# A decode kernel with its backward: the turn between the third and the last cache pass written out by 512 units, and the passes' openings in 1 MB requests

## The chip, the cores and the metric

The kernel runs on one core of a Trainium2 chip. The metric is the time of one execution on the device, in microseconds, as the median of several runs. Engines are called by the profile's names: PE (TensorE, matrix products), DVE (VectorE), ACT (ScalarE), POOL (GpSimd) and SP (SyncE, which here issues the loads).

## The reference

Two layers of a decoder work on one token of width D = 1024, with the same weights. Each layer is an attention over a cache of 65,536 positions (32 query heads, 4 key and value heads, head width 128) and a dense stage with a squared ReLU (F = 3584):

```python
x = x + attention(layernorm(x), k_cache, v_cache, wq, wo)     # softmax(q k / sqrt(128)) v, then wo
x = x + (relu(layernorm(x) @ w1 + b1) ** 2) @ w2 + b2
x = x + attention(layernorm(x), k_cache, v_cache, wq, wo)
x = x + (relu(layernorm(x) @ w1 + b1) ** 2) @ w2 + b2
out, vjp = jax.vjp(f, x, k_cache, v_cache, wq, wo, w1, b1, w2, b2)
return (out, *vjp(grad_out))
```

So the result is the output and the gradients with respect to x, both caches and all weights. The gradients of the caches alone have the caches' size (each cache is 64 MB in bfloat16).

## The kernel before, in words

The kernel reads both caches four times, in four passes numbered 0 to 3: pass 0 is the attention forward of the first layer, pass 1 that of the second, pass 2 the attention backward of the second layer, and pass 3 the backward of the first, which also stores the gradients of the caches. Between the passes lie turns, in which the dense weights are applied: the first turn between passes 0 and 1, the second between 1 and 2 (last forward and first backward through the dense stage), the third between 2 and 3. The code calls layers by L1 and L3 for attention and L2 and L4 for the dense stages.

All loads go into an arena of 20 granules of 1 MB (`Slot`). Some granules hold planes of scores or kept blocks of a cache across a turn, so in the third turn about five are free for weights.

**Cache loads.** A block of a cache is 1 MB. The helper `kv8` (L355 to L372) loads the block that the pass needs next. For an even block it first tries to take two adjacent granules and to load two blocks with one request of 2 MB (L370). If no two adjacent ones are free, or if the block's key stands in `KV["halves"]`, or in pass 3, it loads one block with a request of 1 MB (L365). `start_pass` (L425 to L431) fills that set with the last 8 blocks that the pass touches, and in passes after the first with the first 10. Inside a pass, the order on PE, DVE and ACT is the written one (`tc.manual_schedule`); SP's order of requests is the scheduler's, and each request waits on SP for its granule.

**Background.** Weights for the next head group are loaded and applied beside a pass. `by_group` says after how many items of a pass the work on the next group begins: at a quarter of a group's items (in pass 3, from the second on, 8 items in).

**The backward passes.** For each unit, `vS` multiplies the value block by the gradient of the attention's output (`dOT`), and adds the term of the softmax's backward with a matrix product of `sel2` and `ndt`, which is the first one into that PSUM bank (L1233 in pass 2).

**The turns.** The second turn is written out by hand: w1 comes in chunks of 512 columns of all 1024 rows (`ch_load`, L1674), seven of them, and for each chunk `ch_turn` transposes a part on PE, ACT or DVE copy the transposes out of PSUM (L1696), `ch_spread` (L1703, L1705) lays the 512 values of the hidden gradient out over the partitions, and `ch_dots` (L1712) does the remaining rows as dot products on DVE.

The third turn goes through a queue of rows, class `Rows`. Its `front` (L664 to L690) takes a row chunk of a weight and either forms a dot product on DVE (L673) or transposes it on PE (L682) and copies it out of PSUM with `evac`, on ACT (L161) or DVE (L164), whichever has the lower sum of the costs noted so far. Its `back` (L705 to L717) multiplies the transposed chunk with the vector (L714). Four weights go through it in turn, each as soon as the vector before it is known:

```python
rows.add(PRE["wq3"], DC, R, ..., fin_dx2, inplace=True)                  # dq of the last group -> dx2
rows.add(w2_slabs()[0], FC, DC, lambda: dx2[:], fin_dh2, mix=True, side=side_x4)
rows.add(w1_slabs()[0], DC, FC, lambda: dh2[:], fin_dx1, cols=f_cols, mix=True)
rows.add(wo_slabs(firstg[3])[0], R, DC, lambda: dx1[:], dO_finish(L1, firstg[3]), inplace=True)
rows.run()
```

All of w2 is used for dh2 before w1 is used for dx1. w1 is read by whole rows here. `side_x4` (L1833) uses the same w2 rows for the forward output of the last dense stage (x4). The order on all engines in this turn is the scheduler's. The next pass opens when `dOT` (L948) is there.

Of the kernel before, what the change touches and what calls it, by code (L numbers as in the profile page):

```python
# [16 lines left out]
P = 128  # L17
# [3 lines left out]
def kernel(  # L21
# [69 lines left out]
    def ps_sc(shape, dtype=F32):  # L91
        return PS["pool"].tile(shape, dtype, name="ps_sc", tag="sc", bufs=1 if PS["pass4"] else 2)
# [332 lines left out]
    def start_pass(p):  # L425
        KV["keep"] = plan_keep(p)
        KV["turned"] = KV.get("next", set())
        KV["next"] = set()
        KV["turn"] = {0: "k", 2: "v"}.get(p)
        NOW["pairs"] = p < 3  # L430
        KV["halves"] = set(TOUCH[p][-8:] + (TOUCH[p][:10] if p else []))  # L431

    def f_cols(ap, nb):
        return ap[:, bass.ds(512 * (nb // 4) + nb % 4, P, step=4)]
# [342 lines left out]
    class Background:  # L777
# [35 lines left out]
        def by_group(self, p, gen):  # L813

            order = list(dict.fromkeys(g for g, _ in ITEMS[p]))
            n = len(ITEMS[p]) // G
            for k, g in enumerate(order[1:]):
                self.later.append((k * n + 8 if PS["pass4"] and k else k * n + n // 4, gen(g), g))

        def drain(self):  # L820
            while self.later:
# [376 lines left out]
    def attn_bwd3(p, L, on_group, bg, end=()):  # L1198
        st = ExitStack()
        dspool = st.enter_context(tc.tile_pool(name="b3_ds", bufs=2))  # L1200
        items = ITEMS[p]
        dOpad = vec.tile([P, G, 8, R], BF, name="dOpad")
        nc.vector.memset(dOpad[:], 0.0)
        state = {}
        gfirst = {g: next(c8 for gg, c8 in items if gg == g) for g in range(G)}
        glast = {g: [c8 for gg, c8 in items if gg == g][-1] for g in range(G)}

        def vT(g, c8):
            bg.need(g)
            vb8 = kv8("v", g, c8)  # L1210
            if is_turned("v", g, c8):
                state[("vt", g, c8)] = vb8
            else:
                pt = ps_tr()
                for i in range(8):
                    nc.tensor.transpose(pt[:, i, :], vb8[:, i, :], ident_b[:, :])  # L1216
                kv_done("v", g, c8)
                vt = turned_to("v", g, c8, vb8)
                evac(vt[:, :, :], pt[:, :, :], kind="kta" if c8 % HB // 8 in ACT_VT else "kt")
                state[("vt", g, c8)] = vt  # L1220

        def vS(g, c8):
            if c8 == gfirst[g]:
                nc.vector.tensor_copy(out=dOpad[:, g, 0, :], in_=L["dOT"][:, gsl(g)])
                ndt = dspool.tile([64, HB, R], BF, name="ndt", tag="ndt")
                nc.vector.tensor_copy(out=ndt[:, :, :], in_=L["nd2"][:, gsl(g)].unsqueeze(1).to_broadcast([64, HB, R]))
                state["ndt"] = ndt
            vt = state.pop(("vt", g, c8))
            for i in range(8):
                s = (c8 + i) % HB  # L1230
                if s == 0:
                    state["ps_dp"] = ps_sc([P, HB, R])
                    nc.tensor.matmul(state["ps_dp"][:, :, :].rearrange("p c r -> p (c r)"), lhsT=sel2[:, :],  # L1233
                                     rhs=state["ndt"][:, :, :].rearrange("o c r -> o (c r)"), start=True, stop=False)
                w = min(8, HB - s)
                nc.tensor.matmul(state["ps_dp"][:, s:s + w, :].rearrange("p a b -> p (a b)"), lhsT=vt[:, i, :],
                                 rhs=dOpad[:, g, 0:w, :].rearrange("p a b -> p (a b)"), start=False, stop=(s == HB - 1))
            if is_turned("v", g, c8):
                kv_done("v", g, c8)
            if (c8 + 8) % HB == 0:  # L1240
                c0 = c8 + 8 - HB
                ps_dp = state["ps_dp"]

                def ds():
                    dsT = dspool.tile([P, HB, R], BF, name="dsT", tag="dsT")
                    nc.vector.tensor_tensor(out=dsT[:, :, :], in0=ps_dp[:, :, :], in1=E(1, g, c0, HB), op=ALU.mult)
                    add_load(dve=0.7)
                    state[("ds", g, c0 // HB)] = dsT
                after(1, ds)

        def k8(g, c8):
            kb8 = kv8("k", g, c8)
            dsT = state[("ds", g, c8 // HB)]
            if c8 % SU == 0:
                state["ps_dq"] = ps_acc([P, 8, R])
            ps_dq = state["ps_dq"]
            for i in range(8):
                c = c8 + i
                s = c % HB
                w = min(8, HB - s)  # L1260
                nc.tensor.matmul(ps_dq[:, 0:w, :].rearrange("p a b -> p (a b)"), lhsT=kb8[:, i, :],  # L1261
                                 rhs=dsT[:, s:s + w, :].rearrange("p a b -> p (a b)"),
                                 start=(c % SU == 0), stop=(c % SU == SU - 1), skip_group_check=True)
            kv_done("k", g, c8)
            if (c8 + 8) % SU == 0:
                su = c8 // SU

                def fold():
                    fold_dq(L, g, su, ps_dq[:, 0, :], gfirst[g] // SU == su, glast[g] // SU == su, dspool)
                    if glast[g] // SU == su:  # L1270
                        on_group(g)
                first_at(1, fold)

        start_pass(p)
        with tc.manual_schedule(engines=ORDERED):
            pipeline(items, [(vT, 0), (vS, TLEAD), (k8, B3_LAG)], bg, end)
        st.close()


    def attn_bwd4(p, La, Lb, on_group, bg, stack, end=()):  # L1280
# [75 lines left out]
        def vS(g, c8):  # L1356
# [3 lines left out]
            for i in range(8):  # L1360
                s = (c8 + i) % J
                if s == 0:
                    state["ps_dp"] = ps_sc([P, J, R2])
                    nc.tensor.matmul(state["ps_dp"][:, :, :].rearrange("p c r -> p (c r)"), lhsT=sel2[:, :],
                                     rhs=state["ndt"][:, :].unsqueeze(1).to_broadcast([64, J, R2]), start=True, stop=False)
                w = min(4, J - s)
                nc.tensor.matmul(state["ps_dp"][:, s:s + w, :].rearrange("p a b -> p (a b)"), lhsT=vt[:, i, :],  # L1367
                                 rhs=DOB[:, g, 0:w, :].rearrange("p a b -> p (a b)"), start=False, stop=(s == J - 1))
            if is_turned("v", g, c8):
                kv_done("v", g, c8)  # L1370
                if c8 % J == J - 8 and nexts:
# [326 lines left out]

    def ch_spread(s):

        pg = ps_tr([P, 512], F32)
        for j in range(4):
            nc.tensor.matmul(pg[:, j * P:(j + 1) * P], lhsT=dhb[:, 4 * s + j:4 * s + j + 1].to_broadcast([P, P]), rhs=ident_b[:, :],  # L1703
                             start=True, stop=True)
# [97 lines left out]
    def on3(g):  # L1802
        if g != lastg[2]:
            bg.add(g_dn(L3, dn3, g, g == firstg[2]))
    attn_bwd3(2, L3, on3, bg, [(10, pre_load("wq3", lambda: wq_slabs(lastg[2], 2)))])
    bg.drain()


# [2 lines left out]
    dx2 = vec.tile([P, DC], F32, name="dx2")  # L1811
    dh2 = vec.tile([P, FC], F32, name="dh2")
    dx1 = vec.tile([P, DC], F32, name="dx1")

    def fin_dx2(y):
        dn_finish(dn3, False)(y)
        dxn3 = ln_bwd(dn3[:], L3["n"], L3["rstd"])
        nc.vector.tensor_tensor(out=dx2[:], in0=dx3[:], in1=dxn3[:], op=ALU.add)

    def fin_dh2(y):  # L1820
        nc.vector.scalar_tensor_tensor(out=dh2[:], in0=y, scalar=2.0, in1=L2["r"][:], op0=ALU.mult, op1=ALU.mult)

    def fin_dx1(y):
        dxn = ln_bwd(y, L2["n"], L2["rstd"])
        nc.vector.tensor_tensor(out=dx1[:], in0=dx2[:], in1=dxn[:], op=ALU.add)
    rows = Rows(DENSE["pool"])
    rows.add(PRE["wq3"], DC, R, lambda: L3["dqT"][:, gsl(lastg[2])], fin_dx2, inplace=True)
    x4 = vec.tile([P, DC], F32, name="x4")
    ps_x4 = ps_acc([P, DC, 64])

    def side_x4(kc, slab):
        for nb in range(DC):
            nc.tensor.matmul(ps_x4[:, nb, :], lhsT=d_cols(slab, nb), rhs=L4["gb"][:, kc:kc + 1].to_broadcast([P, 64]),  # L1833
                             start=kc == 0 and nb == 0, stop=kc == FC - 1 and nb == DC - 1, skip_group_check=True)
        add_load(pe=DC * 0.03)
        if kc == FC - 1:
            f = tmp.tile([P, DC], F32, name="ffn_f")
            nc.vector.tensor_tensor(out=f[:], in0=ps_x4[:, :, 0], in1=b2c[:], op=ALU.add)
            nc.vector.tensor_tensor(out=x4[:], in0=x3[:], in1=f[:], op=ALU.add)
            col_to_dram(x4, D, out_0.rearrange("a b d -> (a b d)"))  # L1840
    rows.add(w2_slabs()[0], FC, DC, lambda: dx2[:], fin_dh2, mix=True, side=side_x4)
    rows.add(w1_slabs()[0], DC, FC, lambda: dh2[:], fin_dx1, cols=f_cols, mix=True)
    rows.add(wo_slabs(firstg[3])[0], R, DC, lambda: dx1[:], dO_finish(L1, firstg[3]), inplace=True)
    rows.run()
    dst.close()
    psA_stack.close()

# [90 lines left out]
```

## Time and profile before

| | |
|---|---|
| runs | 1949.32, 1951.35, 1955.88 us; median 1951.35 |
| profiled execution | 1954.17 us; span in the trace 1952.4 us, mean granted clock of TensorE 0.916 |
| busy | PE 82%, DVE 60%, ACT 54%, POOL 7% |
| data moved | 787.63 MB, 403 GB/s on average; 617.62 MB read, 165.69 MB written |
| first turn, us from the span's start | about 350 to 413, pass 1 opens behind it |
| second turn | about 745 to 786, pass 2 opens behind it |
| third turn | about 1128 to 1183, pass 3 opens at 1185.4 and ends at 1946 |
| in the third turn | dq 1127.97, dx2 1136.43, dn2 1177.2, dx1 1179.79, dOT 1183.14 |

The span runs from the first to the last instruction, and the execution's own time is 1.8 us longer. In the profile, a line such as L682 is a line of the kernel; "out<-in" names what an instruction writes and reads; "x152" is a count; and the idle time before a group is given with what ended it. GB/s is what all of the core's DMA engines moved in a stretch, and the DMA share how much of the stretch they were busy.

### The profile page before, as it was taken

The numbers are of one execution on the slowest core, as the hardware profiler recorded it, in microseconds if no ns is written. First come the engines' busy times: TensorE is split into PE (matmuls) and PEld (weight loads), VectorE is DVE, ScalarE is ACT, GpSimd is POOL, SyncE is SP. The second block draws the span as 40 slices with busy tenths as digits, with TensorE's granted clock in tenths as the row PEclk, the third lists the DMA queues.
The fourth block names the chain that finished last, engine by engine and source line by source line (L and its number), as shares of the span: only waits on it lengthen the run. The fifth ranks groups of instructions, "written<-read, shape, count | busy, mean of one in ns | idle before, by whom it ended". The sixth has DMA issues, their size and how long they took to land. (4 is left out here: it accounts for less than half of the span.)

```text
span 1952.4 us, 66978 instructions
## 1 busy us (share of the span) xinstructions
PE 1592.5 (82%) x30199; PEld 1304.0 (67%) x30199; DVE 1172.5 (60%) x2453; ACT 1044.6 (54%) x1617; POOL 141.8 (7%) x321
## 2 busy tenths in 40 slices
PE   6878788688878888877787888889987987787977
PEld 6868778587777777777776885555554554454544
DVE  5645555255545555545464576867875886676866
ACT  3434334254334446435363455766875785676765
POOL 0000000000000000000000001211211211121211
PEclk9999899699899999999899999988996998898997
DMA  9999999999999999899999988999999999899998
GB/s 395 426 426 427 426 428 413 397 398 424 429 425 428 427 423 304 333 425 428 427 423 418 408 309 302 416 405 406 424 423 420 401 424 412 355 423 392 424 422 318
DMA packets 105997, 787.63 MB, mean 403 GB/s; under 512 B 9312, under 2 KB 16494, under 8 KB 42094
## 3 DMA queue, kind: packets, MB, share of 16 engines
q1 hardware_dynamic: 81630, 617.65, 76.8%
q0 software_dynamic: 24080, 165.70, 20.4%
q8 instruction: 236, 3.87, 0.7%
q14 instruction: 51, 0.42, 0.1%
HBM read 617.62 MB, written 165.69 MB: 401 GB/s over the span
## 5 line engine op out<-in xcount | busy, mean ns | idle before, releaser
L164 DVE COPY kt<-ps_tr 128x1024 bf16<-128x1024 bf16 x724 | 497.0, 689 | 438.2 <-PE ps_tr L1024 244.6
L161 ACT CAST arena<-ps_gg 128x1024 bf16<-128x1024 f32 x457 | 444.5, 1011 | 194.7 <-PE ps_gg L1408 145.1
L1024 PE MATMUL ps_tr<-ident_b,arena 128*128 128x128 bf16 x3840 | 309.2, 225 | 32.3 <-DMA arena<-in_A_k_cache_dram 21.0
L164 DVE CAST arena<-ps_gg 128x1024 bf16<-128x1024 f32 (+2 forms) x186 | 222.4, 1196 | 86.4 <-PE ps_gg L1408 41.6
L161 ACT COPY kt<-ps_tr 128x1024 bf16<-128x1024 bf16 x164 | 171.3, 1052 | 186.5 <-PE ps_tr L1216 112.0
L1024 PEld LDWEIGHTS <-arena 128*128 128x128 bf16 x3840 | 233.5, 101 | 39.8 <-DMA arena<-in_A_k_cache_dram 23.4
L1126 PE MATMUL ps_acc<-arena 128*128 128x64 bf16 (+4 forms) x4096 | 205.8, 196 | 64.5 <-DMA arena<-in_A_v_cache_dram 51.9
L1408 PE MATMUL ps_gg<-GG,xt 64*128 64x512 bf16 x1024 | 212.8, 413 | 41.8 <-DVE arena L164 29.1
L1126 PEld LDWEIGHTS <-arena 128*128 128x128 bf16 x4096 | 159.9, 100 | 70.1 <-DMA arena<-in_A_v_cache_dram 55.6
L1336 PE MATMUL ps_tr<-ident_b,arena 128*128 128x128 bf16 x1824 | 178.5, 233 | 32.5 <-DMA arena<-in_A_v_cache_dram 30.5
L1107 ACT ACTIVATE arena<-S_sb,L_negm 128x128 bf16<-128x128 f32 x256 | 165.7, 1005 | 63.7 <-DVE L_negm L1092 63.7
L1042 PE MATMUL ps_sc<-L_qpad,kt 128*128 128x64 bf16 (+7 forms) x3584 | 183.5, 194 | 17.8 <-ACT kt L161 8.9
L1216 PE MATMUL ps_tr<-ident_b,arena 128*128 128x128 bf16 x1920 | 155.4, 227 | 42.6 <-DMA arena<-in_A_v_cache_dram 41.8
L1336 PEld LDWEIGHTS <-arena 128*128 128x128 bf16 x1824 | 118.0, 104 | 88.6 <-issue 54.0
L1042 PEld LDWEIGHTS <-kt 128*128 128x128 bf16 x3584 | 153.0, 100 | 22.6 <-ACT kt L161 11.8
L1216 PEld LDWEIGHTS <-arena 128*128 128x128 bf16 x1920 | 117.9, 102 | 46.6 <-DMA arena<-in_A_v_cache_dram 44.4
L1439 PEld LDWEIGHTS <-arena 128*128 128x128 bf16 x2048 | 95.1, 102 | 61.9 <-issue 42.2
L1107 ACT ACTIVATION_READ_ACCUMULATOR arena<-S_sb,L_negm 128x1 f32 x256 | 128.4, 502 | 0.0
L1408 PEld LDWEIGHTS <-xt 64*128 64x128 bf16 x1024 | 64.6, 94 | 87.9 <-issue 49.4
L587 ACT ACTIVATE mv_t<-mv_t 128x1024 bf16<-128x1024 bf16 x96 | 102.0, 1064 | 36.1 <-DVE mv_t L598 36.0
L1261 PE MATMUL ps_acc<-dsT,arena 128*128 128x64 bf16 (+7 forms) x2048 | 102.9, 194 | 16.1 <-DMA arena<-in_A_k_cache_dram 13.2
L1367 PE MATMUL ps_sc<-DOB,kt 128*128 128x64 bf16 (+3 forms) x1824 | 113.3, 198 | 0.0
(317 smaller groups left out, 2156.9 us busy)
## 6 DMA issues: line engine op xcount, KB each, us to landing
arena<-in_A_k_cache_dram SPq DMA_DIRECT2D x86, 2048.0 KB, 21.3
arena<-in_A_v_cache_dram SPq DMA_DIRECT2D x83, 2048.0 KB, 21.2
out_dram<-arena POOLq DMA_DIRECT2D x149, 1024.0 KB, 17.0
arena<-in_A_v_cache_dram SPq DMA_DIRECT2D x76, 1024.0 KB, 13.7
arena<-in_A_k_cache_dram SPq DMA_DIRECT2D x76, 1024.0 KB, 14.8
arena<-in_A_wo_dram SPq DMA_DIRECT2D x22, 1024.0 KB, 13.9
arena<-in_B_w_dram SPq DMA_DIRECT2D x21, 1024.0 KB, 9.1
arena<-in_A_wq_dram SPq DMA_DIRECT2D x18, 1024.0 KB, 13.6
```

The source lines that it names most:

```text
L161: nc.scalar.copy(out=out, in_=in_)
L164: nc.vector.tensor_copy(out=out, in_=in_)
L587: nc.scalar.activation(out=t[:, :], in_=t[:, :], func=ACTF.Copy, accum_out=y[:, kc:kc + 1])
L1024: nc.tensor.transpose(pt[:, i, :], kb8[:, i, :], ident_b[:, :])
L1042: nc.tensor.matmul(state["ps_s"][:, s:s + w, :].rearrange("p a b -> p (a b)"), lhsT=kt[:, i, :], rhs=L["qpad"][:, g, 0:w, :].rearrange("p ...
L1107: nc.scalar.activation(out=E(p, g, c0, SU)[:, :, h], in_=S[:, h, :], func=ACTF.Exp, bias=L["negm"][:, g, su, h:h + 1], scale=SCALE, accum_ ...
L1126: nc.tensor.matmul(ps_o[:, 0:w, :], lhsT=vb8[:, i, :], rhs=E(p, g, c, w), start=(c % SU == 0), stop=(c % SU == SU - 1), skip_group_check=True)
L1216: nc.tensor.transpose(pt[:, i, :], vb8[:, i, :], ident_b[:, :])
L1261: nc.tensor.matmul(ps_dq[:, 0:w, :].rearrange("p a b -> p (a b)"), lhsT=kb8[:, i, :], rhs=dsT[:, s:s + w, :].rearrange("p a b -> p (a b)") ...
L1336: nc.tensor.transpose(pt[:, i, :], vb8[:, i, :], ident_b[:, :])
L1367: nc.tensor.matmul(state["ps_dp"][:, s:s + w, :].rearrange("p a b -> p (a b)"), lhsT=vt[:, i, :], rhs=DOB[:, g, 0:w, :].rearrange("p a b - ...
L1408: nc.tensor.matmul(pg[:, 512 * h:512 * h + 512], lhsT=xt[64 * h:64 * h + 64, j1 // 8 + m, :], rhs=gg[64 * h:64 * h + 64, :, :].rearrange(" ...
```

## The change

- **Openings.** The list of blocks that passes 1 and 2 load in requests of 1 MB at their start grows from 10 to 18 (pass 3 has no pairs anyway).
- **The later group.** In passes 1 and 2 the background of the first next group begins at a half of the group's items instead of a quarter.
- **Late delta.** In `vS` of passes 2 and 3, for a group's first unit, the product of `sel2` and `ndt` comes last into its bank instead of first.
- **A bank.** `ch_spread` of the second turn takes its PSUM tile from another pool.
- **The third turn.** wq's rows are transposed in place at the end of pass 2 (`turn_wq`, 8 items before the end). The rest is written out in a `manual_schedule`. w2 comes in seven chunks of 512 rows and w1 in seven chunks of 512 columns, and they are loaded in turn, w2 first. For each chunk s, in this order: `back2` and `unite` give 512 values of dh2 (half of them from PE, half from dot products on DVE, and all from PE for the first chunk); `turn2` transposes the next chunk of w2; `spread1`; `dots2` of the next chunk; `back1` adds the chunk's part of dn2 for six of eight row blocks; `turn1` transposes the next chunk of w1, the last part of it copied by DVE; `dots1` does the other two row blocks on DVE; `x4_part` of the next chunk; then the granules are given back and `more` issues the next loads. x4 is finished after the rows of wo.

```diff
-        KV["halves"] = set(TOUCH[p][-8:] + (TOUCH[p][:10] if p else []))
+        KV["halves"] = set(TOUCH[p][-8:] + (TOUCH[p][:18] if p else []))
...
-                self.later.append((k * n + 8 if PS["pass4"] and k else k * n + n // 4, gen(g), g))
+                self.later.append((k * n + 8 if PS["pass4"] and k else k * n + n // (2 if p in (1, 2) and k == 0 else 4), gen(g), g))
...
+                late = c8 + i - s == gfirst[g]
...
+                if s == 0 and not late:
+                    delta(True)
...
+                if s == HB - 1 and late:
+                    delta(False)
...
-        pg = ps_tr([P, 512], F32)
+        pg = ps_acc([P, 512])
...
+    attn_bwd3(2, L3, on3, bg, [(10, pre_load("wq3", lambda: wq_slabs(lastg[2], 2))), (8, turn_wq)])
...
+    ND = 2
+    loads = deque((k, s) for s in range(NCH) for k in "21")
+
+    def more():
+        while loads and FREE:
+            k, s = loads.popleft()
+            sl = Slot("s_w%sd" % k)
+            if k == "2":
...
+                nc.sync.dma_start(out=v, in_=f_rows_of(B_w2)[:, s, :, :])
...
+            else:
...
+                nc.sync.dma_start(out=v, in_=rows_of(B_w1)[:, :, 512 * s:512 * s + 512])
...
+    def fin_dn3(y):
         dn_finish(dn3, False)(y)
-        dxn3 = ln_bwd(dn3[:], L3["n"], L3["rstd"])
+
+        def between():
+            turn2(0, 0)
+            turn2(0, 1)
+        dxn3 = ln_bwd(dn3[:], L3["n"], L3["rstd"], between)
         nc.vector.tensor_tensor(out=dx2[:], in0=dx3[:], in1=dxn3[:], op=ALU.add)
-    rows = Rows(DENSE["pool"])
-    rows.add(PRE["wq3"], DC, R, lambda: L3["dqT"][:, gsl(lastg[2])], fin_dx2, inplace=True)
-    rows.add(w2_slabs()[0], FC, DC, lambda: dx2[:], fin_dh2, mix=True, side=side_x4)
-    rows.add(w1_slabs()[0], DC, FC, lambda: dh2[:], fin_dx1, cols=f_cols, mix=True)
-    rows.add(wo_slabs(firstg[3])[0], R, DC, lambda: dx1[:], dO_finish(L1, firstg[3]), inplace=True)
-    rows.run()
...
+    with tc.manual_schedule(engines=ORDERED):
+        wq_in_place.run()
+        more()
...
+        back2(0)
+        unite(0)
...
+        for s in range(NCH):
+            last = s == NCH - 1
+            if s:
+                back2(s)
+                unite(s)
+            if not last:
+                for j in range(on_pe(s + 1)):
+                    turn2(s + 1, j)
+            spread1(s)
+            if not last:
+                dots2(s + 1)
+            back1(s)
+            if not last:
+                for j in range(3):
+                    turn1(s + 1, j)
+            dots1(s)
+            if not last:
+                turn1(s + 1, 3, True)
+            if s == 0:
+                x4_part(0)
+                w2c.pop(0)[0].free()
+            if not last:
+                x4_part(s + 1)
+                w2c.pop(s + 1)[0].free()
+            w1d.pop(s)[0].free()
+            more()
...
+        dxn1 = ln_bwd(dn2[:], L2["n"], L2["rstd"], wo_turn)
+        nc.vector.tensor_tensor(out=dx1[:], in0=dx2[:], in1=dxn1[:], op=ALU.add)
+        rows.begin(job)
+        wo_turn()
+        next(wo_rows, None)
+        rows.run()
+        f4 = tmp.tile([P, DC], F32, name="ffn_f")
...
+        col_to_dram(x4, D, out_0.rearrange("a b d -> (a b d)"))
```

## The prediction

> **What bounds the kernel now.** I read the page first (busy shares, then the forty slices), then the DMA rate window by window around the three turns, then SP's timeline and PE's waits in the opening that looks worst, and last the groups of instructions inside the turns. The page:
>
> ```profile
> PE 1592.5 (82%) x30199; PEld 1304.0 (67%) x30199; DVE 1172.5 (60%) x2453; ACT 1044.6 (54%) x1617; POOL 141.8 (7%) x321
> ...
> GB/s 395 426 426 427 426 428 413 397 398 424 429 425 428 427 423 304 333 425 428 427 423 418 408 309 302 416 405 406 424 423 420 401 424 412 355 423 392 424 422 318
> DMA packets 105997, 787.63 MB, mean 403 GB/s; under 512 B 9312, under 2 KB 16494, under 8 KB 42094
> ```
>
> No compute engine is full, and most slices move 423 to 429 GB/s. At 425, 787.63 MB take 1853 us of the 1952.4: the transfers set the pace, and some 100 us are time in which they did not run at that rate. The two deepest dents are slices 16 and 17 (second turn, 732 to 830 us) and 24 and 25 (third turn, 1123 to 1220). So what an edit is worth is how much DMA time it wins or loses there. Stretches (columns: window, length, busy time of each engine, granted clock, DMA share, GB/s):
>
> ```profile
> 410.00:420.00 10.00, 8.19 (x228) 7.95 (x228) 2.37 (x8) 1.17 (x2) 0.00 (x0) 0.83 0.81 312
> 760.00:765.00 5.00, 4.69 (x114) 4.42 (x114) 3.81 (x14) 3.42 (x6) 0.00 (x0) 1.00 0.95 303
> 785.00:795.00 10.00, 8.77 (x198) 8.22 (x199) 5.62 (x13) 4.05 (x4) 0.00 (x0) 1.00 0.97 391
> 795.00:805.00 10.00, 10.00 (x276) 9.07 (x273) 5.01 (x9) 6.03 (x10) 0.00 (x0) 1.00 0.24 70
> 1140.00:1160.00 20.00, 17.05 (x400) 16.09 (x396) 15.61 (x36) 14.18 (x17) 1.16 (x11) 1.00 0.91 334
> 1350.00:1390.00 40.00, 36.51 (x449) 22.20 (x448) 30.37 (x59) 30.18 (x34) 7.61 (x15) 0.91 1.01 424
> ```
>
> The fourth line is a hole: 70 GB/s in ten microseconds, PE full. SP's timeline shows why, and PE pays behind it:
>
> ```profile
> 789.70 0.33 SPq L365 DMA_DIRECT2D arena<-in_A_v_cache_dram  x1
> 802.32 0.33 SPq L370 DMA_DIRECT2D arena<-in_A_k_cache_dram  x1
> ```
> ```profile
> PE ps_acc L1261 <- DMA arena<-in_A_k_cache_dram: 4.7, 1, 4.7
> PE ps_sc L1233 <- DVE ndt L1226: 1.3, 1, 1.3
> ```
>
> The last 1 MB request (L365) goes out at 789.70; the next one is a pair (L370), which needs two adjacent granules free at once, and they are free only at 802.32.
>
> **Openings.** The opening list grows from 10 to 18 blocks in the second and third pass, so the next eight requests are singles, each sent when one granule comes free. By the order of releases (one for every 32 of the opening's matmuls) they go out between 787 and 803 and the queue stays filled. At 424 the hole 795 to 805 could have moved 4.24 MB and moved 0.70: 8.4 us lost; with 785 to 795, 9.1. The lower bound is what PE waited, 4.7. I take 8, near the lost bytes, since it is the transfers that bound the pass behind it. The second pass's opening has a smaller dent of the same kind (312 GB/s in 410 to 420: 2.6 us lost; SP sends a k single at 404.39, then nothing until the pair at 415.79): I take 2.5, bounds 0 and 2.6. Eight singles in place of four pairs also mean four more issues of 0.33 us on SP, which waits for granules anyway: nothing, and 1.3 us if SP had no slack.
>
> Does a 1 MB request cost rate? The window 1350:1390 lies in the last pass, where pairs are off and every cache block is a 1 MB request: 424 GB/s, as in passes with pairs. [...]
>
> **The later group.** For the second and third pass, wq and wo loads of the next head group start at half of the group instead of a quarter. The bytes are the same and lie in a stretch at 425 GB/s either way; nothing. If the second half were too short for them they would run in a block at the group's change, at most a few us.
>
> **Late delta.** In a group's first unit the sel2 x ndt matmul moves from first to last. PE waited 1.3 us for ndt at L1233 (above), so between 0 and 1.3 gained; there the DMA comes last, and the gain is already in the 8: nothing. In the last pass's opening the first score matmul waits for dOT, not for ndt, so nothing there either. The bank of ch_spread (second turn): 0 to 0.3 us, nothing.
>
> **The third turn.** Removed: the Rows queue, which ran wq's matmuls, x4's sums and the transposes of w2 interleaved. Rows used (core's groups inside the turns; busy, mean ns):
>
> ```profile
> L161 ACT COPY wt<-ps_tr 128x1024 bf16<-128x1024 bf16 x15 | 14.8, 1018 | 8.1 <-PE ps_tr L682 8.0
> L673 DVE SCALAR_TENSOR_TENSOR mv_junk<-arena,vbc 128x1024 bf16<-128x1024 bf16 x11 | 12.7, 1218 | 0.0
> ```
> ```profile
> L1696 ACT COPY wt<-ps_tr 128x640 bf16<-128x640 bf16 x17 | 10.9, 706 | 1.0 <-PE ps_tr L1694 1.0
> L1705 ACT CAST wvb<-ps_tr 128x512 bf16<-128x512 f32 x6 | 3.5, 586 | 8.9 <-issue 5.5 <-PE ps_tr L1703 3.4
> ```
>
> Ahead of it, wq's 64 transposes and 8 copies in place (before mostly at 1119.4 to 1123, as the tail of the pass) now start 8 items before the pass's end, in its written order: 3.5 us of PE and some 7 us of copies, beside DVE at 44% and ACT at 26% (1110 to 1120), so nothing; with no such cover at most the 3.5 of PE.
>
> Head. Before, dq is done at 1127.97, wq's 64 matmuls end at 1134.34 because other work lies between them, and dx2 is there at 1136.43. Written in one piece the 64 take 2.15 us (as the 64 of wo did at 1180.95), so dx2 comes at about 1132.7, 3.7 us earlier. Behind it come the cast, back2(0), unite, the row form of dx2 and the first transposes: with the small steps of this stage, the loop starts at about 1137.7.
>
> Body. Per 512 units: PE has 40 transposes at 0.054 us (24 take 1.50 with their drain, 16 take 1.07), 72 matmuls at 0.034 and the spread, 4.85 us; ACT two copies of 1.02, one cast of 0.59 and three copies of 768 columns, 0.81 each between the 640 and 1024 rows, 5.06; DVE two dots of 1024 (1.15 from start to start), two of 512 (0.61), a copy of 768 (0.55) and the unite (0.5), 4.6. They hide in one another except where PE, in its written order, must do x4, back2 and turn2 between ACT's last evacuation of one body and the first of the next: I take 5.9 a body. The last body has no next chunk: 3.8.
>
> Loads. A row chunk at 425 GB/s takes 2.47 us. The column chunk is read in runs of 1 KB, as in the second turn, where the full DMA moves 303 at a share of 0.95, or 319: 3.3 us. Seven of each: 40.4 us instead of 34.6, so 5.8 us of extra DMA time, 5.8 a body, just under the body. [...]
>
> Stall. Five granules are free; the first five loads end at about 1140.5, and the next slots come free late in body 0 (about 1142). In SP's order the column chunk 3 then stands ahead of column chunk 2, though chunk 2 is needed first. A column load alone took 5.17 us from issue to landing (757.59 to 762.76); with a second behind it, chunk 2 lands at 1142 + 5.2 + 3.3 = 1150.5, and body 1 wants it about 3.5 us in, at 1147.1: 3.4 us. What is queued behind PE's wait: the rest of the turn's copies, x4 and the next body; behind the load on SP: all later chunks, wo and the next pass's k.
>
> End: 1137.7 + 5.9 + (5.9 + 3.4) + 4 x 5.9 + 3.8 = 1180.3; from dn2 to dx1 2.6 and to dOT 3.35 as before (1177.2, 1179.79, 1183.14): 1186.2, which is 3.1 later than before. Bounds: -4 (no stall, body 5.4) to +9 (stall 6.5, body 6.3).
>
> The last pass's opening: x4's final sums and transposes now stand ahead of the first score matmuls on PE: 0.4, between 0 and 0.5. The prefetch of k is as before, so a shift of dOT reaches the end in full.
>
> **Sum**, against the profiled run of 1954.17 (span 1952.4 and 1.8 around it): -8 - 2.5 + 3.1 + 0.4 = -7.0, or 1947.2. The median of the runs is 0.14% below the profiled one: 1944.4. What measurement can tell from no change is 0.3%, 5.9 us.
>
> **Rivals.**
> (A) Slower: the third turn starves. During a body three granules hold data in use, and two are left for the next chunk. Released at the end of a body, a row load lands 4.7 us later (1164.90 to 1169.62) and a column load behind it 3.3 later still, 8.0; the first is wanted after 5.9, the second after 9.4, which fits. If the column load goes out ahead of the row load in every body, as it does once already, and runs at the 281 GB/s of 765 to 770 (3.7 us), the row chunk lands after 8.4: 2.5 us in each of five bodies, and the first stall grows by 3.1. Turn +18.7, total +8.6, median about 1960. It decides from a landing 2 us late in every body. For: SP's order and the 1 KB runs; against: only one such inversion is seen in the order.
> (B) The hole moves: when pairs resume after 18 blocks, SP waits once more for two adjacent granules, and up to all of the 10.5 us return. For: the pass before has the same wait at its tenth block; against: by then the releases run ahead of the loads. [...] Total between -2 and +3.5, median about 1952.
> (C) No stall in the turn, body 5.4, and the 3.7 us of dx2 carry through: turn -4, total -14, median about 1937.
>
> **How the numbers follow.** Forecast 0.45, A 0.17, B 0.23, C 0.15. Faster by over 0.3% is C, most of the forecast (its spread of 3 us reaches above the bound) and a little of B: 0.58. Same: most of B and the upper tail of the forecast, 0.25. Slower 0.17, nearly all A. The range 1935 to 1958 takes in C, B and A's lower end.
>
> **What would show it.** In the trace after: no gap of over 5 us between SP's cache requests in the third pass's opening, the window ten to twenty microseconds after its start above 380 GB/s, PE's L1261 wait of 4.7 gone; the second opening above 400. In the third turn, dx2 about 4.8 us behind dq, one PE or DVE wait on the column load of 3 to 4 us in body 1, bodies of 5.9 us, dOT about 3 us later against dq than before (55.2 us). The forecast is wrong if a hole of over 5 us stands behind the 18th block, or if the waits on B_w in the turn sum to over 10 us.

## The result: slower by 0.8%

The changed kernel takes 1970.7 us (median of six runs; one of them, at 3246 us, is left out of the comparison) against 1955.8 for the kernel before, run beside it: ratio 1.0082, 95% interval 1.006 to 1.0104, by which it is some 16 us slower. Forecast were 1944.4, 7 us faster, and a range from 1935 to 1958. The profiled execution took 1969.17 us with a span of 1967.4.

The page of the kernel after, busy shares and rates of the forty slices:

```profile
PE 1587.4 (81%) x30190; PEld 1303.4 (66%) x30190; DVE 1170.3 (59%) x2476; ACT 1045.1 (53%) x1623; POOL 140.4 (7%) x297
...
GB/s 388 423 421 420 424 424 409 388 403 420 424 421 424 424 412 299 386 421 425 422 418 417 398 260 258 407 425 398 424 424 417 406 424 416 355 417 395 424 422 333
DMA packets 113277, 787.63 MB, mean 400 GB/s; under 512 B 9424, under 2 KB 23774, under 8 KB 48350
```

Two things stand out. The second turn's dent is shallower (slice 17: 333 before, 386 now), and the third turn's is deeper (slices 24 and 25: 309 and 302 before, 260 and 258 now). A smaller difference is easy to miss: slices 2 to 6, far ahead of any edit, read 420 to 424 where they read 426 to 428 before.

Windows of the kernel after (window, length, busy of each engine, granted clock, DMA share, GB/s); the pass behind the second turn opens 9 us later than before, so its hole at 795 to 805 would lie at 804 to 814 here (419 GB/s in that window too):

```profile
410.00:420.00 10.00, 7.91 (x181) 7.45 (x179) 2.61 (x16) 2.21 (x3) 0.00 (x0) 0.83 0.97 356
795.00:805.00 10.00, 10.00 (x236) 9.40 (x234) 5.77 (x10) 5.06 (x5) 0.00 (x0) 1.00 0.98 389
800.00:810.00 10.00, 9.09 (x255) 8.69 (x255) 3.84 (x6) 2.02 (x2) 0.00 (x0) 1.00 1.01 419
1130.00:1140.00 10.00, 9.14 (x201) 9.07 (x199) 6.18 (x16) 0.07 (x1) 0.00 (x0) 0.88 0.54 193
1140.00:1160.00 20.00, 13.16 (x282) 12.23 (x278) 12.00 (x35) 12.62 (x16) 0.00 (x0) 0.99 0.83 293
```

The hole of 70 GB/s behind the second turn is gone (389 and 419). The hole now is in the third turn, around the last dq: 193 GB/s with PE and DVE busy and ACT idle, where the kernel before moved 360 (1121 to 1131).

Cutting each trace at four kinds of events makes the traces comparable: the last attention result of a forward pass, the first and the last dOT or dq of a backward one. "Pass 1" has the first turn in it, and turn 3 runs from the last dq of pass 2 to the first dOT of pass 3. Lengths in us, each from one profiled execution:

| kernel | pass 0 | pass 1 | turn 2 | pass 2 | turn 3 | pass 3 |
|---|---|---|---|---|---|---|
| before | 369.7 | 377.2 | 37.4 | 343.5 | 55.4 | 751.4 |
| before, again (e1) | 370.0 | 378.7 | 39.9 | 344.9 | 54.0 | 748.0 |
| after | 374.0 | 381.7 | 38.0 | 343.2 | 64.2 | 748.5 |
| openings alone (e2) | 369.6 | 377.0 | 39.7 | 337.6 | 56.4 | 745.3 |
| turn alone (e3) | 373.9 | 383.6 | 38.5 | 352.4 | 61.5 | 746.2 |
| after, w1 chunk 2 first (e5) | 374.3 | 382.1 | 40.1 | 345.0 | 55.7 | 745.4 |
| after, arena as before (e6) | 370.1 | 379.5 | 39.7 | 340.3 | 61.2 | 751.3 |
| before, arena 64 bytes lower (e7) | 374.2 | 382.1 | 40.1 | 349.3 | 56.5 | 749.4 |
| e6 and x4 moved (e8) | 369.5 | 377.5 | 39.5 | 339.9 | 50.1 | 744.7 |
| e8 and wq earlier (e9) | 369.5 | 376.3 | 38.3 | 338.0 | 51.7 | 746.7 |
| e9 with other loads for w1 (e10) | 370.0 | 378.1 | 38.6 | 340.8 | 52.3 | 746.7 |
| openings alone, again (e13) | 369.8 | 377.2 | 40.0 | 336.6 | 55.9 | 747.3 |
| 18 singles alone (e11) | 369.8 | 376.1 | 38.3 | 336.2 | 58.6 | 748.6 |
| before, arena 128 bytes lower (e12) | 373.8 | 383.8 | 37.4 | 347.0 | 55.6 | 750.6 |

Pass 0 says most: no edit touches it, it repeats to 0.6 us, and it falls into two groups, 369.5 to 370.1 and 373.8 to 374.3.

### The profile page after: what moved, and what is told of

It reads as the page before. It is cut to its first block, busy times and chain, and to the rows that moved or that the text cites. A ratio compares the mean times of both kernels' runs of the same rounds, so it can differ in the third digit from the quotient of the medians.

```text
span 1967.4 us, 66963 instructions
## 1 busy us (share of the span) xinstructions
PE 1587.4 (81%) x30190; PEld 1303.4 (66%) x30190; DVE 1170.3 (59%) x2476; ACT 1045.1 (53%) x1623; POOL 140.4 (7%) x297
## 5 line engine op out<-in xcount | busy, mean ns | idle before, releaser
L1354 POOL COPY xin<-arena 128x512 bf16<-128x512 bf16 x64 | 39.5, 617 | 1286.6 <-DMA arena<-in_A_k_cache_dram 1193.9
```

## The experiments

### Which part, and is it the run or the kernel? (e1, e2, e3)

e1 is the kernel before, unchanged. e2 is before with all edits but the third turn's, e3 is after without them.

> The kernel before once more, for a trace beside the next ones. In the trace of after, pass 0 (no edit touches it) ended 4.3 us later than in the trace of before, and turn 1 with pass 1 was 4.5 us longer. Theory S (starved turn): that is the chip of that run, so here too pass 0 ends near 374 us and pass 1 near 755 if the chip is the same, and not otherwise than in the other traces of this set. Theory P (the passes pay for the openings in 1 MB requests and the later group): here pass 0 ends at about 370 as in the first trace of before, and the kernels with the openings edit end it and pass 1 later.

> Before, with all edits but those of the third turn (18 singles, later group, late delta, the bank). Theory S: faster than before by 3 to 9 us (ratio 0.995 to 0.9985), the hole behind the second turn gone, turn 3 55 us as before. Theory P: slower by 5 us or more, and slower than before already at the end of pass 1.

> After without the openings, the later group, the late delta and the bank: the third turn's rewrite alone. Theory S: slower than before by 15 to 22 us (all of the loss and what the openings gain), turn 3 from the last dq to dOT about 64 us instead of 55.4, the last dq itself some 4 us later against the pass, as PE does the 64 transposes of wq ahead of the last 56 dq matmuls. Theory P: slower by 5 us at most.

Measured: e1 took 1955.2 us, as before. e2 0.9941 (0.9921 to 0.9961), so 11.5 us faster. e3 1.012 (1.0096 to 1.0144), 23 us slower. So the openings gain and the turn's rewrite costs, as theory S had it, and both by a little more than its ranges. But its account of pass 0 was wrong: in one set on one chip, pass 0 took 370 us in e1 and e2 and 374 in e3 and e5. The rewrite of the third turn slows a pass that ends over 750 us before the turn begins. Theory P, which blamed the openings for it, falls too: e2 has the openings and a pass 0 of 369.6.

### What slows pass 0? (e6, e7, e12)

The rewrite does away with the row queue's tile `rows_y` (two buffers of 32 bytes per partition), since its result now goes into `dn2`, which shares the buffers of `lnb_pr`. The pool `tmp` is 64 bytes shorter, and every pool allocated behind it moves down by as much, in all parts of the program. The arena starts at byte 48832 of each partition instead of 48896. The old start is 191 times 256, the new one 192 over a multiple of 256, and all twenty granules move with it, as each is 8 KB wide.

```diff
# e6: after
-        dn2 = tmp.tile([P, DC], F32, name="dn2", tag="lnb_pr")
+        dn2 = tmp.tile([P, DC], F32, name="dn2")
# e7: before
-                    ys = tmp.tile([P, nk], F32, name="rows_y")
+                    ys = tmp.tile([P, nk], F32, name="rows_y", tag="lnb_pr")
# e12: as e7, and
-        gb2 = tmp.tile([P, DC], F32, name="gb2")
+        gb2 = tmp.tile([P, DC], F32, name="gb2", tag="ffn_f")
```

> After, with one tile (dn2) in a buffer of its own, 64 bytes per partition more in the pool tmp, no instruction more or less. The allocation then puts the arena at byte 48896 of each partition as in before (a multiple of 256) instead of 48832. Theory G (granule address): every load into the arena runs about 1.1% slower from 48832, as passes 0 to 2 show (pass 0 374 us in all three kernels with the turn's rewrite, 370 in all three without); so pass 0 ends at 370, passes 1 and 2 are 4 to 5 us shorter each, and the total is 10 to 13 us less than after (2 to 5 over before). Rival I (the instruction stream or something else in the rewrite slows the passes): pass 0 stays at 374, total as after.

> Before, with one tile (rows_y) sharing another's buffer, 64 bytes per partition less in the pool tmp, no instruction more or less; the arena starts at 48832. Theory G: slower than before by 9 to 13 us (ratio 1.005 to 1.007), pass 0 at 374 us. Rival I: as before, within 2 us, pass 0 at 370.

> Before with 128 bytes per partition less in the pool tmp (two tiles share buffers with others; one small DVE instruction is issued a few places later), the arena at 48768, which is 128 over a multiple of 256. If any start off a multiple of 256 costs the same: as with 48832, pass 0 at 374 and 14 to 18 us slower than before. If only odd multiples of 64 cost: pass 0 at 370, as before.

Measured: e6 1.002 (1.0006 to 1.0034), e7 1.0087 (1.0063 to 1.0111), e12 1.0074 (1.0051 to 1.0097). The kernel before becomes 17 us slower by a move of 64 bytes, more than theory G's 9 to 13, and after wins back 12 us of its 16. The intervals of 12, 14.5 (e12) and 17 overlap. The rate in 300 us of pass 0, in e6 and then in e7:

```profile
40.00:340.00 300.00, 242.07 (x5759) 232.11 (x5757) 164.73 (x369) 131.67 (x319) 0.00 (x0) 0.95 1.01 425
```
```profile
40.00:340.00 300.00, 242.63 (x5633) 232.19 (x5630) 161.43 (x364) 127.14 (x308) 0.00 (x0) 0.93 1.00 421
```

The DMA is as busy (share 1.01 and 1.00) and moves 1% less; before has the 425 of e6 in this window, and after the 421 of e7. This is what theory G said, and rival I falls. 128 over a multiple of 256 (e12, 1.0074) costs the same as 192 over (e7, 1.0087), within the intervals.

The pools between `tmp` and the arena moved too, so one may ask whether it is the loads. In the traces it is: between 40 and 340 us the packets of the loads take longer, those of 16 KB 618.9 ns on average in e7 against 615.1 in e6 (621.6 in after, 617.0 in before), while the copies into `kt`, whose pool moved by the same 64 bytes, take 690 ns on DVE in before and after alike.

### Is it the order of two loads, or the late release? (e5, e8)

```diff
# e5: after, in the loop's first body
             if s == 0:
+                w1d.pop(s)[0].free()
+                more()
                 x4_part(0)
...
# e8: e6, and x4_part(0) with its free() and more() ahead of the loop
             back1(s)
             if not last:
+                x4_part(s + 1)
+                w2c.pop(s + 1)[0].free()
+                more()
                 for j in range(3):
                     turn1(s + 1, j)
```

> After, with column chunk 2 put into the granule that comes free first, so that it goes out ahead of column chunk 3. Theory S with the inversion as its core: PE's wait of 5.95 us in body 1 falls to about 1.5 to 3 and the total is 4 us less than after (about 12 over before). Theory S with the late release as its core (the granules come free only at the end of body 0, whatever the order): 1.5 us less at most, the wait stays over 4. Theory P: as after.

> After, with the arena at 48896 and x4_part moved: chunk 0 ahead of the loop, chunk s+1 between back1 and turn1, with the w2 granule given back and the next load issued there. Theory S (late release of granules starves the loop): the waits on B_w in the turn, 5.95 and 2.43 us on PE, fall to under 2 together, turn 3 from the last dq to dOT 54 us or less (64.2 in after), total 8 to 11 less than the aligned kernel beside it, some 6 us faster than before. If the stalls come from the 1 KB runs (the load itself too slow), the turn stays over 60 us.

What they were to mend, in the kernel after: PE's waits between 1120 and 1200 us (us in total, times, longest), then PE in body 1 of the loop, then SP:

```profile
PE ps_tr L1885 <- DMA arena<-in_B_w_dram: 5.9, 1, 5.9
PE ps_acc L1270 <- DMA arena<-in_A_k_cache_dram: 4.0, 1, 4.0
PE ps_tr L1885 <- ACT w1t L1887: 3.1, 5, 0.7
PE ps_tr L1872 <- DMA arena<-in_B_w_dram: 2.4, 1, 2.4
```
```profile
1154.33 0.91 PE L1945 MATMUL ps_bg<-dhb,w1t 128*128 128x64 bf16 x24
1161.19 2.75 PE L1885 MATMUL ps_tr<-ident_b,arena 128*128 128x128 bf16 x24 [5.95 <-DMA arena<-in_B_w_dram]
```
```profile
1139.48 0.33 SPq L1857 DMA_DIRECT2D arena<-in_B_w_dram  x1
1151.05 1.25 SPq L1861 DMA_DIRECT2D arena<-in_B_w_dram  x2
```

SP sends nothing for 11.6 us, then column chunks 3 and 2 in that order (landed at 1156.62 and 1161.14). PE stands until the second of the two, chunk 2, is there, although the first, chunk 3, is not needed before body 2.

e5: 1.0052 (1.0035 to 1.007), 6 us less than after, and turn 3 is 55.7 instead of 64.2. PE's one wait of 5.9 has become five of 1.3 at most:

```profile
PE ps_tr L1885 <- DMA arena<-in_B_w_dram: 4.0, 5, 1.3
```

So the order of two loads was worth some 6 us, near the 4 that theory S gave it, and the late release alone, by which the wait would have stayed over 4, falls. e8: 0.9961 (0.9943 to 0.9979), some 11 us less than e6, 8 less than before. The waits on B_w are gone from PE's list, and turn 3 takes 50.1 us, less than either kernel's. SP in e8 sends the next column chunk 5 us behind the fifth load instead of 11.6:

```profile
1128.99 0.33 SPq L1857 DMA_DIRECT2D arena<-in_B_w_dram  x1
1134.14 0.38 SPq L1861 DMA_DIRECT2D arena<-in_B_w_dram  x1
```

It also shortened the body itself: from one conversion of dh2 (L1929) to the next, bodies without a stall take 5.64 us in after (1172.49 to 1178.13) and 5.12 in e8 (1142.42 to 1147.54). In e8 x4's matmuls stand ahead of `turn1` and no longer between two bodies, and ACT's idle time before w2's copies falls from 29.0 us in after to 18.0, of which 17.4 lie ahead of the first copy; that this is the reason was not tested apart. e8 releases granules earlier and moves x4 in one edit, so it does not say what share each has.

### Transposes of wq ahead of the last dq (e9)

```diff
-[(10, pre_load("wq3", ...)), (8, turn_wq)]
+[(16, pre_load("wq3", ...)), (10, turn_wq)]
```

> As the x4 kernel beside it, and wq's rows loaded 16 steps before the pass's end instead of 10 and transposed 10 steps before instead of 8, so that they lie in PE's wait for the last k block (3.97 us at L1270 in after) and not ahead of the last 56 dq matmuls. Theory S with the wq part: 3 to 5 us less than the x4 kernel, the last dq that much earlier against the pass's start. If the last k block lands late anyway: the same within 1 us, with the wait moved behind the transposes.

Its reason, in PE's timeline of the kernel after:

```profile
1129.55 0.61 PE L1270 MATMUL ps_acc<-dsT,arena 128*128 128x64 bf16 x8 [3.97 <-DMA arena<-in_A_k_cache_dram]
1129.97 1.90 PE L682 MATMUL ps_tr<-ident_b,arena 128*128 128x128 bf16 x16
...
1134.24 0.61 PE L682 MATMUL ps_sc<-ident_b,arena 128*128 128x128 bf16 x8
```

PE waits 4 us for a block of k, then does the transposes for 4.7 us (with DVE copying all of them), and only then the last 56 matmuls of dq, which also hold the granules that the turn's second and third load wait for. Measured: 0.9948 (0.9932 to 0.9964), not told apart from e8. Pass 2 is 1.9 us shorter and turn 3 1.6 longer. The 3 to 5 us expected did not come: a miss. The edit did not do what it was for either. In e9's trace the transposes still stand behind PE's wait for the block of k, not in it:

```profile
1113.66 1.46 PE L1270 MATMUL ps_acc<-dsT,arena 128*128 128x64 bf16 x24 [1.46 <-DMA arena<-in_A_k_cache_dram]
1114.93 1.90 PE L682 MATMUL ps_tr<-ident_b,arena 128*128 128x128 bf16 x16
```

In e10, which has the same order in this pass, that wait is 3.1 us. So what transposes inside the wait would be worth, no run here shows.

### Does the column load's rate set the turn? (e10)

> As the kernel with x4 and wq moved (arena at 48896), but each w1 column chunk of 1 MB (runs of 1 KB) is replaced by a load of 1 MB of w2 rows (runs of 8 KB) into the same granule at the same place in the order, so dx1 and what follows from it come from other data. Theory R (the column runs still set the turn): turn 3 shorter by 3 to 6 us (51.7 now), total by the same. Theory S (once the granules are released early, loads lie under the bodies' 5.6 us): turn 3 within 1.5 us, total within 2.

```diff
-                nc.sync.dma_start(out=v, in_=rows_of(B_w1)[:, :, 512 * s:512 * s + 512])
+                nc.sync.dma_start(out=sl.t[:, :].rearrange("p (j n) -> p j n", j=4), in_=f_rows_of(B_w2)[:, s, :, :])
```

This kernel computes other values for dx1 and what follows from it, so only its time is of use. Measured: 0.9954 (0.9938 to 0.9971), turn 3 52.3 us against 51.7 in e9. With granules released early the 1 KB runs cost nothing that shows, as theory S had it.

### Which opening edit? (e11, e13)

e11 changes only the 10 to 18; e13 is e2 once more.

> Before with 18 singles in place of 10 and nothing else (no later group, no late delta, no other bank). If the holes of the openings are the whole gain: as the kernel with all the openings edits beside it, 10 to 13 us faster than before. If the late delta and the later group carry part: 5 to 8 us faster, pass 2 340 us or more instead of 337.6.

> The openings edits alone once more, beside the others: about 12 us faster than before, pass 1 with its turn 377, pass 2 338. Against the kernel with the mended turn it tells whether the rewrite of the turn is worth anything: the traces so far say 4 us for the mended rewrite (span 1943.5 against 1938.9).

Measured: e11 0.9964 (0.9951 to 0.9976), 7 us faster; e13 0.9953 (0.9937 to 0.997), 9 us. Pass 2 took 336.2 and 336.6. The singles carry most of it. What the later group and the late delta add, 0 to 5 us, is not resolved: e11's pass 2 is no longer than those of e2 and e13, although PE's wait of 1.3 us on ndt is still in e11's list (L1233), which speaks against a gain there. Against the openings alone (e13) the mended rewrite (e9) gives no gain that the ratios tell: 0.9948 and 0.9953, with the intervals overlapping, though its turn 3 is 4 us shorter.

## Why the prediction was wrong, point by point

**The openings: right behind the second turn, open behind the first.** Forecast 8 in the third pass; pass 2 fell from 343.5 and 344.9 to 337.6, 336.6 and 336.2, so 7.4. Forecast 2.5 in the second pass; measured 1.2 (377.2 and 378.7 to 377.0, 377.2 and 376.1), less than the two kernels before differ by. The dent itself is filled: 410 to 420 reads 421 GB/s in e2, whose pass 0 ends as in before, where it read 312. SP's requests and PE's waits behind the second turn in the kernel after:

```profile
793.68 0.33 SPq L365 DMA_DIRECT2D arena<-in_A_v_cache_dram  x1
796.25 0.33 SPq L365 DMA_DIRECT2D arena<-in_A_k_cache_dram  x1
```
```profile
PE ps_acc L1270 <- issue: 1.7, 1, 1.7
PE ps_mv L953 <- DVE dlt_prod L950: 0.5, 1, 0.5
```

Between 793.68 and 815.28 SP sends nine singles of the caches, at most 6.7 us apart and there with a load of wo between, and the waits of 4.7 us on k and 1.3 on ndt are gone from the list of that stretch. Rival B was there in small: between the last single (815.28) and the first pair (824.46) SP sends nothing for 9 us. By the words of the prediction, a hole of over 5 us behind the 18th block, this was a sign against the forecast; but the rate falls only to about 370 for 10 us, 1.3 us of DMA time. The filled queue moved 419 GB/s from 800 to 810, in single requests.

**The step that failed most is not in the sum at all.** The prediction took all durations outside the edited places as given, which puts the allocation at nothing. The allocation moved the arena by 64 bytes, and that cost 12 us (after against e6) to 17 us (e7 against before). It lies in passes 0 to 2, 4 to 5 us in each on average (e7 and e12 against before and e1); pass 3, which stores while it loads, shows no difference (749.4 and 750.6 in e7 and e12, 751.4 and 748.0 in before and e1). The working looked at the order of instructions and never at the addresses. Without the move the time would have lain in the range (e6: 1957), but not on the side that was forecast: e6 is 1 to 7 us slower than before, where 7 faster stood.

**The turn: the mechanism was right, its size not.** Forecast +3.1; measured 64.2 against 55.4 and 54.0, so about 9 to 10 (6 to 7 in e3 and e6). Step by step, in us behind the last dq: dx2 at 4.5 (forecast 4.8). The body without a stall 5.64 (5.9), ACT's copies of 768 columns at 0.83 where 0.81 was assumed:

```profile
L1887 ACT COPY w1t<-ps_tr 128x768 bf16<-128x768 bf16 x22 | 16.4, 829 | 7.8 <-PE ps_tr L1885 7.8
L1877 ACT COPY w2t<-ps_tr 128x1024 bf16<-128x1024 bf16 x15 | 14.4, 1018 | 29.0 <-DVE lnb_pr L252 17.8 <-PE ps_tr L1872 11.2
L1902 DVE SCALAR_TENSOR_TENSOR mv_junk<-arena,vbc 128x1024 bf16<-128x1024 bf16 x12 | 14.2, 1220 | 2.0 <-DMA arena<-in_B_w_dram 1.9
```

The stall in body 1, foreseen with its cause, made the body 13.1 us long, 7.5 over a free one, where 3.4 were forecast. PE's wait in it is 5.95. The release was priced right: the next column load goes out 14 us behind dq in the forecast and in the trace. Mis-sized was the landing: chunk 2 was taken to land 8.5 us behind the first of the two issues and took 10.1, with a row load sent 1 us behind them (1152.91). PE also wanted it 0.8 us sooner than forecast, and the rest of the 7.5 is overlap that was lost behind the wait.

A second stall, in body 4 (9.2 us, 3.6 over), was not in the sum. It is rival A's condition: a column load goes out just ahead of the row load, and PE waits for the row chunk.

```profile
1170.83 0.37 SPq L1861 DMA_DIRECT2D arena<-in_B_w_dram  x1
1171.73 0.34 SPq L1857 DMA_DIRECT2D arena<-in_B_w_dram  x1
```
```profile
1180.26 1.89 PE L1872 MATMUL ps_tr<-ident_b,arena 128*128 128x128 bf16 x16 [2.43 <-DMA arena<-in_B_w_dram]
```

From the issue of the row load to the end of PE's wait are 8.5 us, and PE lost 2.4; rival A priced 8.4 and 2.5, but in each of five bodies, and it came in one.

**wq's transposes: not free.** They were put down to nothing, for the idle ACT and DVE, with 3.5 us as the cost without cover. Pass 2 is 340.3 in e6 and 339.9 in e8, against 336.8 on average in the kernels without the rewrite but with the singles: 3.3 us. In the kernel before the 64 transposes fill PE's wait for the last blocks of k:

```profile
1119.44 1.05 PE L682 MATMUL ps_tr<-ident_b,arena 128*128 128x128 bf16 x16
1123.84 1.11 PE L1261 MATMUL ps_acc<-dsT,arena 128*128 128x64 bf16 x32 [0.47 <-DMA arena<-in_A_k_cache_dram]
1126.26 1.06 PE L1261 MATMUL ps_acc<-dsT,arena 128*128 128x64 bf16 x32 [1.31 <-DMA arena<-in_A_k_cache_dram]
```

In the kernel after PE waits 3.97 us first and transposes then, as the timeline at e9 shows. So the cover that counted was not idle time on DVE and ACT but PE's own wait, and the written order gave it up. This is read from the traces and not shown by a run: e9 and e10 kept the transposes behind the wait, and their passes 2 (338.0 and 340.8) differ by nearly as much as the effect.

**The last pass's opening: in its range by luck.** Forecast were 0.4 for x4's sums and nothing for the late delta, since the first score matmul was said to wait for dOT and not for ndt. From dOT to the first score matmul pass 2.61 us before (1183.14 to 1185.75), with the product of ndt ahead of it, and 2.73 now (1201.07 to 1203.80): +0.1. But with the late delta and without the rewrite (e2 and e13) it is 0.9:

```profile
1181.27 1.06 PE L1382 MATMUL ps_sc<-DOB,arena 128*128 128x64 bf16 x32 [0.25 <-DVE negd L956]
```

So the late delta took 1.7 us off this stretch and x4's sums put 1.8 back. Whether 1.7 us there reach the end of the pass, these runs do not tell.

Together, without the move of the arena: -7.4 - 1.2 + 6.6 (e3 and e6) + 3.3 + 0.1 = +1.4, where e6, which is just this kernel, measured +4 (1 to 7). The arena's 12 on top of e6 gives the 16.

## What to carry to other kernels

When a kernel is bound by transfers, compare the start addresses of its big buffers before and after an edit; a tile that disappears in one pool moves all that is allocated behind it (64 bytes cost 12 to 17 us here), and a stage that no edit touches is the control that shows it (pass 0 here, 374 us against 370). In a loop fed by few buffers, price a load by all that is in flight beside it (chunk 2 took 10.1 us to land here, where 8.5 were forecast), put the work that releases a buffer as early as its inputs allow, and see that the loads go out in the order of need (e8, which also moves x4, took some 11 us less than e6, and the order alone was worth some 6, e5). Openings with small requests that need only one free buffer were a cheap gain here, where the queue otherwise waited for two adjacent ones (7 us, e11).

## What the runs showed of the hardware

Loads in pass 0, which go mostly in packets of 16 KB (117.5 of 127.5 MB between 40 and 340 us in before; 16 KB is what a pair puts into one partition), ran at 421 GB/s into an arena that starts at byte 48832 or 48768, 192 or 128 over a multiple of 256, against 425 from 48896, which is such a multiple, at nearly the same DMA share (1.00 and 1.01); in time, 374 against 370 us for pass 0, 1.1%. Counted by bytes, the 135 MB that follow the first 10 took 318.9 to 319.1 us in six traces with the old start and 321.9 to 322.3 in five with the others. The single packet is longer by about 4 ns at each of three sizes: 615.1 and 618.9 ns for 16 KB, 309.7 and 313.9 for 8 KB, 84.5 and 88.1 for 2 KB (means between 40 and 340 us, e6 and e7; in before and after 617.0 and 621.6, 310.3 and 314.1, 84.5 and 88.0). In pass 3 the loads of 8 KB take 309 ns in the median with both starts, where in pass 0 before and after have 309 and 312, so the start does not cost everywhere; why not there is open.

What a packet spends the 4 ns on is not seen in a trace. Three starts were run, and the one that is a multiple of 256 was the fast one; whether that is the reason, three starts do not tell.
